# Splitting the diagonal score blocks of a causal attention at 64 queries, and running the matching part of PV as 64-row tiles

## Chip, cores, metric

One core of a Trainium2 chip. The metric is the device time of one execution in microseconds (us), median of several. Times are of fast runs, with a granted TensorE clock of about 1.00. Ratios are the mean time of one kernel's fast runs over the mean of the other's fast runs of the same rounds, so they are not quite the ratio of the medians that I quote.

## The reference, cut to what matters

Sequence 2048, width 512, 32 heads of 16, in four segments of 512 tokens. Each segment does causal softmax attention within itself and reads a linear memory of the earlier segments; a gated FFN of width 1792 runs beside it on the same input.

```python
for s in range(4):                                   # L = 512
    logits = einsum('bhqd,bhkd->bhqk', qs, ks) * scale + mask   # causal within the segment
    a_dot  = einsum('bhqk,bhkd->bhqd', softmax(logits), vs)
    a_mem  = (phi(qs) @ M) / (phi(qs) @ z + 1e-6)
    outs.append(g * a_mem + (1 - g) * a_dot)
    M, z = M + phi(ks).T @ vs, z + phi(ks).sum(...)
a = concat(outs) @ wo
b = (relu(x @ W_gate) * (x @ W_up)) @ W_down
return g2 * a + (1 - g2) * b                         # g2 = sigmoid(x . gate_w)
```

## The kernel before

A static list scheduler in the kernel (with a random seed) orders every operation on every engine beforehand; at run time each engine follows its fixed list and waits on semaphores. FFN and projection matmuls fill PE between the steps of the attention.

Heads come in groups of eight (G). The transposed keys of one parity p of a head pair are kept with the other parity zeroed (`kp`), so that four tiles of 32 rows compute four heads at once. A "quad" is one set of scores of four heads by 512 columns, in four PSUM banks, followed by one exp of 2048 elements a partition:

```python
def quad(tag, parts):                       # parts: (n, key block j, column offset, width)
    for (n, j, o, w) in parts:
        for jj in range(4):
            q.matmul(PL[:, jj, o:o + w], lhsT=V.kp[32*jj:32*jj+32, kslot(s, n), 128*j:128*j+128],
                     rhs=V.qT[32*jj:32*jj+32, qslot(s, n//2), 128*j:512], tile_position=(32*jj, 0), ...)
    a.activation(V.E[:, e, :, :], PL[:, :, :], ACT.Exp, scale=SCALE)           # ScalarE
    for o in offsets:                                                         # GpSimd, 4 x 128 a partition
        g.affine_select(out=V.E[:, e, :, o:o+128], ...)                        # causal mask of the diagonal block
...
# five quads per G: key blocks of 128 keys see 512, 384, 256, 128 queries
eA[0] = quad("A0", [(n0, 0, 0, 512)]);  eB[0] = quad("B0", [(n0, 1, 0, 384), (n0, 3, 384, 128)])
eC    = quad("C",  [(n0, 2, 0, 256), (n1, 2, 256, 256)])
eA[1] = quad("A1", [(n1, 0, 0, 512)]);  eB[1] = quad("B1", [(n1, 1, 0, 384), (n1, 3, 384, 128)])
```

PV of a group comes as a pair, one per parity, with V and a column of ones as the stationary operand, in four tiles of 32 columns:

```python
src = [(eA[p], 0, 512, 0), (eB[p], 0, 384, 128), (eC, 256*p, 256, 256), (eB[p], 384, 128, 384)]
for j, (e, o, w, c) in enumerate(src):
    for jj in range(4):
        q.matmul(A(ep)[32*jj:32*jj+17, c:512], lhsT=V.vaug[:, s % 2, j, 8*G + 2*jj + p, :],
                 rhs=V.E[:, e, jj, o:o+w], tile_position=(0, 32*jj), ...)
```

The softmax here doesn't subtract the row's maximum and nothing guards it: scores larger than these inputs give would overflow.

Of the kernel before, what the change touches and what calls it, by code (L numbers as in the profile page):

```python
# [9 lines left out]
ALU = mybir.AluOpType  # L10
# [78 lines left out]
class Sched:  # L89
# [90 lines left out]

    def _bank_choice(self, op, e):
        cls = op.ep.cls
        if cls != "att":
            held = 0
            nheld = 0
            for prev in self.bank_ep:
                if prev is None or all(r.done for r in prev.readers):
                    continue
                held += prev.cls == cls
                nheld += 1  # L190
            if held >= self.CAPS.get(cls, 2) or nheld >= len(self.bank_ep) - 1:
                return None
        best = None
        for bi, prev in enumerate(self.bank_ep):
            if prev is not None and not all(r.done for r in prev.readers):
                continue
            ft = self._bank_free(prev, e)
            if best is None or ft < best[1]:
                best = (bi, ft)
        return best  # L200
# [166 lines left out]
def plan(S, D, F):  # L367
# [4 lines left out]
        ("qT", [128, 8, 512], BF16), ("kT", [128, 4, 512], BF16), ("kp", [128, 12, 512], BF16),  # L372
        ("phiq", [128, 4, 512], BF16), ("ek", [128, 4, 512], BF16), ("phik", [128, 4, 512], BF16), ("ttmp", [128, 2, 512], BF16),
        ("vaug", [128, 2, 4, 32, 17], BF16), ("E", [128, 8, 4, 512], BF16),
        ("Tn", [128, 2, 512], F32), ("adT", [128, 512], BF16), ("oTt", [128, 512], BF16),
        ("amem", [128, 2, 512], BF16), ("amemT", [128, 4, 512], BF16), ("oT", [128, 8, 512], BF16),
        ("hT", [128, 20, 512], BF16), ("rl", [128, 3, 512], BF16), ("osb", [128, 3, 512], BF16),
# [3 lines left out]
        ("rden", [128, 32], F32), ("rdg", [128, 32], F32), ("rdm", [128, 128], F32), ("pm8", [128, 8], F32), ("pm", [128, 2], F32), ("ident", [128, 128], BF16),  # L381
# [3 lines left out]
def build_kernel(nc, A_x, A_wq, A_wk, A_wv, A_wo, A_beta, W_g, W_u, W_d, gate_w, out):  # L385
# [5 lines left out]
    sc = Sched(seed=59)  # L391
# [14 lines left out]
def program(sc, nc, T, PL, PA, A_x, A_wq, A_wk, A_wv, A_wo, A_beta, W_g, W_u, W_d, gate_w, out, NSEG, KT, NF, NT, EPS, SCALE):  # L406
# [13 lines left out]

    def act(fn, occ, **k):
        return op("act", fn, occ, **k)
# [20 lines left out]
    for nm, w, src in (("wq", V.wq, A_wq), ("wk", V.wk, A_wk), ("wv", V.wv, A_wv)):  # L443
        for kt in range(KT):
            load("act" if nm == "wq" and kt % 2 == 0 else "sp", [f"{nm}{kt}"], w[:, kt, :], src[kt * 128:(kt + 1) * 128, :], 1 << 17)
    load("act", ["gwb"], V.gwb[:], gate_w.partition_broadcast(128), 1 << 17)
# [52 lines left out]
    ds.append(dve(lambda e: e.reduce_sum(V.pm[:, :], pm8, AX.X), 180, reads=["pm8"], writes=["pm"], name="pm"))  # L499
    sc.queue(0, ds)  # L500
# [29 lines left out]
    for s2 in range(2):  # L530
        for tt in range(4):
            cst.append(dve(lambda e, s2=s2, tt=tt: e.tensor_copy(V.vaug[:, s2, tt, :, 16], V.romgh[:, :]), 190, reads=["romgh"], writes=[f"vone{s2}_{tt}"], name="vone"))
# [4 lines left out]
    gq = {"pe": [], "act": [], "dve": [], "flex": [], "pool": [], "sp": []}  # L537
    for c in range(NSEG):
# [17 lines left out]
        gexpT_r[c] = []  # L556
        for a in range(4):
            for jj in range(4):
                dst = V.gexpT[32 * jj:32 * jj + 32, 16 * c + 4 * a:16 * c + 4 * a + 4]
                gq["flex"].append(sc.add(Op([("dve", lambda e, a=a, dst=dst, t0=t0, t1=t1: e.tensor_copy(dst, V.gexp[32 * a:32 * a + 32, t0:t1]), 200),  # L560
                                             ("act", lambda e, a=a, dst=dst, t0=t0, t1=t1: e.activation(dst, V.gexp[32 * a:32 * a + 32, t0:t1], ACT.Copy), 215)],
                                            reads=[f"gexp{c}"], writes=[f"gexpT{c}_{a}{jj}"], name="gexpT")))
                gexpT_r[c].append(f"gexpT{c}_{a}{jj}")
# [8 lines left out]
    sc.queue(2, gq["flex"])  # L572
    sc.queue(3, gq["sp"])

    def kslot(s, n):
        return (s * 8 + n) % 12
# [11 lines left out]
    def proj(s):  # L588
# [3 lines left out]
        def pj(w, col, name, wname, tokmajor=False):  # L592
            ep = Epoch("proj")

            step = 1 if s == 0 and name == "q" and col < 2 else 2
# [9 lines left out]
            return ep  # L605
        for G in range(4):
            ep = pj(V.wq, G, "q", "wq")
            qs = qslot(s, G)
            evs.append(dve(lambda e, ep=ep, qs=qs: e.tensor_copy(V.qT[:, qs, :], A(ep)[:, :]), t_dve(512), writes=[f"qT{qs}"], name=f"qcp{s}_{G}", ep=ep, role="r"))  # L609
# [3 lines left out]
            evs.append(dve(lambda e, ep=ep, G=G: e.tensor_copy(V.kT[:, G, :], A(ep)[:, :]), t_dve(512), writes=[f"kT{G}"], name=f"kcp{s}_{G}", ep=ep, role="r"))  # L613
            for p in range(2):
                ks = kslot(s, 2 * G + p)
                km = lambda e, G=G, p=p, ks=ks: e.tensor_scalar(V.kp[:, ks, :], V.kT[:, G, :], V.pm[:, p:p + 1], None, ALU.mult)  # L616
                ka = lambda e, G=G, p=p, ks=ks: e.activation(V.kp[:, ks, :], V.kT[:, G, :], ACT.Copy, scale=V.pm[:, p:p + 1])
                evs.append(sc.add(Op([("dve", km, 420)] + ([("act", ka, 720)] if s else []), reads=[f"kT{G}", "pm"], writes=[f"kp{ks}"], name=f"kmask{s}_{G}_{p}")))
# [4 lines left out]
        for tt in range(4):  # L623
            ep = pj(V.wv, tt, "v", "wv", True)
            evs.append(dve(lambda e, ep=ep, tt=tt: e.tensor_copy(V.vaug[:, s % 2, tt, :, 0:16], A(ep)[:, :].rearrange("q (h c) -> q h c", c=16)), t_dve(512), writes=[f"va{s % 2}_{tt}"], name=f"vcp{s}_{tt}", ep=ep, role="r"))
        if s == 0:
            pes = [p for k in "qkv" for p in pes if p.name[0] == k]
            pes[:2 * KT] = [pes[h * KT + kt] for kt in range(KT) for h in range(2)]
        return pes, evs, sbs, acts, sps

    def va(s):
        return [f"va{s % 2}_{tt}" for tt in range(4)] + [f"vone{s % 2}_{tt}" for tt in range(4)]

    def mu(s):
        pes, ds, ps = [], [], []
        for hf in range(2):
            ep = Epoch()

            def fn(e, hf=hf, ep=ep):
                for g in range(2):  # L640
                    G = 2 * hf + g
                    for tt in range(4):
                        ins = e.matmul(A(ep)[:, g * 136:(g + 1) * 136], lhsT=V.phik[:, tt, G * 128:(G + 1) * 128], rhs=V.vaug[:, s % 2, tt, 8 * G:8 * G + 8, :], start=(tt == 0), stop=(tt == 3))  # L643
# [38 lines left out]
    e_ctr = [0]  # L682

    carry = []

    def att(s, between):
        pes, acts, pools, ds, pvs = [], [], [], [], []

        def quad(tag, parts):
            e = e_ctr[0]  # L690
            e_ctr[0] = (e + 1) % 8
            wid = max(o + w for (_, _, o, w) in parts)
            assert wid == 512

            def fq(q, parts=parts):
                for (n, j, o, w) in parts:
                    for jj in range(4):
                        ins = q.matmul(PL[:, jj, o:o + w], lhsT=V.kp[32 * jj:32 * jj + 32, kslot(s, n), 128 * j:128 * j + 128],  # L698
                                       rhs=V.qT[32 * jj:32 * jj + 32, qslot(s, n // 2), 128 * j:512], start=True, stop=True, tile_position=(32 * jj, 0), skip_group_check=True)
                return ins  # L700
            rd = [f"kp{kslot(s, n)}" for (n, _, _, _) in parts] + [f"qT{qslot(s, n // 2)}" for (n, _, _, _) in parts]
            pes.append(pe(fq, sum(mm(w) for (_, _, _, w) in parts), reads=rd, writes=[f"bankL{b}" for b in range(4)], name=f"quad{s}_{tag}", mode="r"))
            acts.append(act(lambda a, e=e: a.activation(V.E[:, e, :, :], PL[:, :, :], ACT.Exp, scale=SCALE), t_act(2048), reads=[f"bankL{b}" for b in range(4)], writes=[f"E{e}"], name=f"exp{s}_{tag}"))  # L703
            for o in [o for (_, _, o, _) in parts]:
                ap = V.E[:, e, :, o:o + 128]
                pools.append(pool(lambda g, ap=ap: g.affine_select(out=ap, in_=ap, compare_op=ALU.is_ge, fill=0.0, base=0, pattern=[[0, 4], [1, 128]], channel_multiplier=-1),  # L706
                                  t_pool(512), reads=[f"E{e}"], writes=[f"E{e}m{o}"], name=f"mask{s}_{tag}"))
            return e

        def flush():  # L710
            if not carry:
                return []
            s, G, eA, eB, eC = carry.pop()
            eps = []
            pair = []
            for p in range(2):
                ep = Epoch("att")
                eps.append(ep)

                def fpv(q, p=p, ep=ep):  # L720
                    src = [(eA[p], 0, 512, 0), (eB[p], 0, 384, 128), (eC, 256 * p, 256, 256), (eB[p], 384, 128, 384)]
                    for j, (e, o, w, c) in enumerate(src):
                        for jj in range(4):
                            ins = q.matmul(A(ep)[32 * jj:32 * jj + 17, c:512], lhsT=V.vaug[:, s % 2, j, 8 * G + 2 * jj + p, :], rhs=V.E[:, e, jj, o:o + w],  # L724
                                           start=(j == 0), stop=(j == 3), tile_position=(0, 32 * jj), skip_group_check=True)
                    return ins
                pair.append(pe(fpv, mm(1280), reads=[f"E{x}" for x in (eA[p], eB[p], eC)] + [f"E{eA[p]}m0", f"E{eB[p]}m0", f"E{eB[p]}m384", f"E{eC}m{256 * p}"] + va(s), name=f"pv{s}_{G}_{p}", ep=ep, role="w", mode="c"))
# [15 lines left out]
            else:  # L743
                ds.append(dve(lambda e: e.transpose(V.oTt[:, :], V.adT[:, :]), t_dve(512), reads=["adT"], writes=["oTt"], name=f"bt{s}_{G}"))
                ds.append(dve(lambda e: e.tensor_tensor(V.oT[:, os_, :], V.oTt[:, :], V.amemT[:, G, :], ALU.add), 540, reads=["oTt"] + [f"amemT{i}" for i in range(4)], writes=[f"oT{os_}"], name=f"oa{s}_{G}"))
            return pair

        for G in range(4):
            n0, n1 = 2 * G, 2 * G + 1
            eA, eB = [None, None], [None, None]  # L750
            eA[0] = quad(f"{G}A0", [(n0, 0, 0, 512)])
            eB[0] = quad(f"{G}B0", [(n0, 1, 0, 384), (n0, 3, 384, 128)])
# [3 lines left out]
            eC = quad(f"{G}C", [(n0, 2, 0, 256), (n1, 2, 256, 256)])  # L756
# [176 lines left out]
```

## Time and profile before

| | before |
|---|---|
| time, median | 273.18 us (272.69 to 273.54) |
| span of the profiled run | 271.2 us |
| PE / VectorE / ScalarE / GpSimd busy | 97% / 76% / 75% / 37% |

In the profile PE is TensorE, PEld its weight loads, ACT ScalarE, DVE VectorE and POOL GpSimd. Lines of the page of the kernel before: the busy time of each engine, PE's row over 40 slices, the chain that ended last, and groups of instructions (count, then busy us and mean ns, then idle time before them and its cause).

```profile
span 271.2 us, 5268 instructions
PE 263.0 (97%) x2108; PEld 115.1 (42%) x2143; DVE 204.8 (76%) x382; ACT 203.7 (75%) x210; POOL 99.5 (37%) x156
...
PE   8989999999999999999999999999999999999996
...
PE 88%; ACT 2%; DVE 2%; DMA 2%; issue 2%; POOL 2%; ACTq 1%; DVEq 0%; POOLq 0%
...
L703 ACT ACTIVATE E<-psL 128x2048 bf16<-128x2048 f32 x80 | 150.0, 1875 | 31.1 <-PE psL L698 30.6
L706 POOL TENSOR_SCALAR_AFFINE_SELECT E<-E 128x512 bf16<-128x512 bf16 x128 | 85.4, 685 | 139.6 <-ACT E L703 139.5
```

PE stands at 9, 90% or more, in every slice from the fourth to the last but one, and is 88% of the chain. But a busy PE is not one at its peak, so I went to the starts of the matmuls. Matmul ends are modelled in a trace and overlap; the distance from one start to the next is what an operation costs. This is PE's timeline around one quad and one PV pair of the kernel before (start, length, line, count):

```profile
91.40 1.03 PE L819 MATMUL psA<-wd,hT 128*128 128x512 bf16 x4
92.36 0.40 PE L698 MATMUL psL<-qT,kp 32*128 32x384 bf16 x8
92.69 1.26 PE L724 MATMUL psA<-E,vaug 128*17 128x512 bf16 x32
94.11 0.81 PE L819 MATMUL psA<-wd,hT 128*128 128x512 bf16 x3 [0.16 <-issue]
```

The quad starts at 92.36 and the PV pair at 92.69, 0.33 us later, although the quad streams only 512 columns. (Full-array matmuls of 128 and 512 columns start 56 and 216 ns apart, so a column costs 0.417 ns and 512 columns 213 ns; all streaming times below are worked out with this.) The last full matmul before a quad takes 312 ns to the next start instead of 216. So each quad costs 0.33 + 0.096 = 0.43 us. The FFN matmul recorded at 94.11 is the second one after the pair (35 of the 2143 matmul records are missing; I filled them in from the weight load that follows each, which is always there).

Adding up all start-to-start distances gives a ledger of PE, in us. A stall is the part of a distance above the median of its kind:

| PE from the first projection to the last matmul | before |
|---|---|
| full-array matmuls, memory update and read-out | 207.58 |
| 80 quads: entry 96 ns, then 327 to 330 ns | 33.94 |
| 16 PV pairs: 1206 ns | 19.25 |
| stalls (of these over 25 ns each: 0.98, both before 18 us) | 1.47 |
| **sum** | **262.24** |

There is almost nothing on PE but work.

### The profile page before, as it was taken

The page shows a single profiled execution, that of the slowest core. Times are in us where ns is not written, and L with a number is a line of the kernel's source. Part 1 is how long each engine was busy: PE and PEld are TensorE (multiplying, and loading weights), DVE is VectorE, ACT ScalarE, POOL GpSimd, SP SyncE. Part 2 cuts the span into 40 slices and gives each one's busy share as a digit, 9 for nine tenths or more (in the row PEclk, how much of TensorE's full clock was granted, in tenths as well). Part 3 has the DMA queues.
Part 4 walks back from the last instruction along what each step waited for, and adds up shares of the span by engine and source line. Part 5 has one row for each costly group of instructions (what it writes and reads, how often), then busy time and mean ns, then how long its engine had stood idle before and what let it go on. Part 6 is the DMA issues. An engine that isn't in the chain of part 4 may idle for free.

```text
span 271.2 us, 5268 instructions
## 1 busy us (share of the span) xinstructions
PE 263.0 (97%) x2108; PEld 115.1 (42%) x2143; DVE 204.8 (76%) x382; ACT 203.7 (75%) x210; POOL 99.5 (37%) x156
## 2 busy tenths in 40 slices
PE   8989999999999999999999999999999999999996
PEld 4433343444444444444343444343434444344444
DVE  4689988899889799999888887877773547776300
ACT  3499998898989987899768779887776768682122
POOL 5614343454533253643333532333333242421000
PEclk9999999999999999999999999999999999999999
DMA  6999953102200143210001220000012000000011
GB/s 192 331 365 238 237 96 69 29 7 55 55 25 19 31 89 97 60 39 2 0 2 39 62 78 22 19 2 1 2 39 52 27 19 22 0 0 4 0 39 41
DMA packets 31017, 17.01 MB, mean 63 GB/s; under 512 B 20880, under 2 KB 30992, under 8 KB 30992
## 3 DMA queue, kind: packets, MB, share of 16 engines
q1 hardware_dynamic: 30272, 16.01, 23.3%
q10 hardware_dynamic: 720, 0.66, 1.0%
q8 instruction: 17, 0.28, 0.4%
q14 instruction: 8, 0.07, 0.1%
HBM read 9.84 MB, written 2.10 MB: 44 GB/s over the span
## 4 chain that ended last, share of the span: by engine, by line
PE 88%; ACT 2%; DVE 2%; DMA 2%; issue 2%; POOL 2%; ACTq 1%; DVEq 0%; POOLq 0%
PE psA L780 36%; PE psA L819 17%; PE psL L698 9%; PE psA L602 8%; PE psA L724 7%; PE psA L812 5%; PE psA L600 4%; DMA gwb<-in_gate_w_dram 2%; POOL Tn L543 2%; PE psA L672 1%; PE psA L643 1%; ACT E L703 1%; ACTq L439 1%; DVE osb L828 1%; PE psA L659 0%
## 5 line engine op out<-in xcount | busy, mean ns | idle before, releaser
L703 ACT ACTIVATE E<-psL 128x2048 bf16<-128x2048 f32 x80 | 150.0, 1875 | 31.1 <-PE psL L698 30.6
L706 POOL TENSOR_SCALAR_AFFINE_SELECT E<-E 128x512 bf16<-128x512 bf16 x128 | 85.4, 685 | 139.6 <-ACT E L703 139.5
L780 PE MATMUL psA<-xT,wg 128*128 128x512 bf16 x213 | 58.0, 380 | 1.1 <-issue 0.8
L780 PE MATMUL psA<-xT,wu 128*128 128x512 bf16 x217 | 58.4, 380 | 0.6 <-issue 0.3
L819 PE MATMUL psA<-wd,hT 128*128 128x512 bf16 (+2 forms) x233 | 53.0, 367 | 0.8 <-issue 0.8
L791 DVE TENSOR_TENSOR hT<-psA,rl 128x512 bf16<-128x512 f32 x56 | 38.2, 683 | 13.5 <-PE psA L780 12.5
L698 PE MATMUL psL<-qT,kp 32*128 32x384 bf16 (+3 forms) x512 | 31.7, 301 | 0.8 <-DVE kp L616 0.5
L780 PEld LDWEIGHTS psA<-xT,wu 128*128 128x128 bf16 x224 | 20.4, 98 | 25.8 <-issue 3.2
L819 PEld LDWEIGHTS psA<-wd,hT 128*128 128x128 bf16 x238 | 20.9, 98 | 23.8 <-issue 4.0
L780 PEld LDWEIGHTS psA<-xT,wg 128*128 128x128 bf16 x224 | 20.1, 98 | 24.9 <-issue 3.1
L729 DVE STREAM_TRANSPOSE Tn<-psA 128x512 f32<-128x512 f32 x32 | 20.9, 692 | 7.9 <-PE psA L724 7.9
L789 DVE TENSOR_SCALAR rl<-psA 128x512 bf16<-128x512 f32 x30 | 20.6, 688 | 4.0 <-PE psA L780 3.0
L698 PEld LDWEIGHTS psL<-qT,kp 32*128 32x128 bf16 x512 | 8.9, 92 | 34.0 <-ACT E L703 14.0
L788 ACT ACTIVATE rl<-psA 128x512 bf16<-128x512 f32 x26 | 15.5, 595 | 10.3 <-PE psA L780 10.2
L724 PE MATMUL psA<-E,vaug 128*17 128x256 bf16 (+3 forms) x512 | 20.2, 300 | 0.0
L829 ACT ACTIVATE osb<-psA,omg 128x512 bf16<-128x512 f32 (+2 forms) x10 | 6.4, 645 | 13.7 <-PE psA L812 13.1
L812 PE MATMUL psA<-wo,oT 128*128 128x512 bf16 (+2 forms) x64 | 15.9, 366 | 0.3 <-issue 0.2
L602 PE MATMUL psA<-xT,wk 128*128 128x512 bf16 x62 | 15.9, 380 | 0.2 <-DVE ttmp L585 0.2
L602 PE MATMUL psA<-xT,wq 128*128 128x512 bf16 x61 | 15.5, 380 | 0.5 <-issue 0.3
L600 PE MATMUL psA<-wv,xT 128*128 128x512 bf16 x61 | 14.7, 380 | 0.4 <-issue 0.3
L724 PEld LDWEIGHTS psA<-E,vaug 128*17 128x17 bf16 x512 | 10.7, 90 | 9.4 <-issue 2.5
L609 DVE CAST qT<-psA 128x512 bf16<-128x512 f32 x16 | 10.7, 676 | 3.4 <-PE psA L602 3.3
(71 smaller groups left out, 233.0 us busy)
## 6 DMA issues: line engine op xcount, KB each, us to landing
out_dram<-osb SPq DMA_DIRECT2D x15, 128.0 KB, 1.7
wg<-in_B_W_gate_dram SPq DMA_DIRECT2D x8, 224.0 KB, 5.4
wu<-in_B_W_up_dram SPq DMA_DIRECT2D x8, 224.0 KB, 5.7
wd<-in_B_W_down_dram SPq DMA_DIRECT2D x1, 1792.0 KB, 10.5
osb<-in_A_x_dram SPq DMA_DIRECT2D x12, 128.0 KB, 2.0
wk<-in_A_wk_dram SPq DMA_DIRECT2D x4, 128.0 KB, 5.6
wv<-in_A_wv_dram SPq DMA_DIRECT2D x4, 128.0 KB, 4.9
wo<-in_A_wo_dram SPq DMA_DIRECT2D x1, 512.0 KB, 5.0
```

The source lines that it names most:

```text
L600: ins = e.matmul(A(ep)[:, :], lhsT=V.xT[:, kt, tok + col * 128:tok + (col + 1) * 128], rhs=w[:, kt, :], start=(kt == 0), stop=(kt == KT - 1))
L602: ins = e.matmul(A(ep)[:, :], lhsT=w[:, kt, col * 128:(col + 1) * 128], rhs=V.xT[:, kt, tok:tok + 512], start=(kt == 0), stop=(kt == KT - 1))
L698: ins = q.matmul(PL[:, jj, o:o + w], lhsT=V.kp[32 * jj:32 * jj + 32, kslot(s, n), 128 * j:128 * j + 128], rhs=V.qT[32 * jj:32 * jj + 32, q ...
L703: acts.append(act(lambda a, e=e: a.activation(V.E[:, e, :, :], PL[:, :, :], ACT.Exp, scale=SCALE), t_act(2048), reads=[f"bankL{b}" for b i ...
L706: pools.append(pool(lambda g, ap=ap: g.affine_select(out=ap, in_=ap, compare_op=ALU.is_ge, fill=0.0, base=0, pattern=[[0, 4], [1, 128]], c ...
L724: ins = q.matmul(A(ep)[32 * jj:32 * jj + 17, c:512], lhsT=V.vaug[:, s % 2, j, 8 * G + 2 * jj + p, :], rhs=V.E[:, e, jj, o:o + w], start=(j ...
L729: ds.append(dve(lambda e, p=p, ep=eps[p]: e.transpose(V.Tn[:, p, :], A(ep)[:, :]), t_dve(512), writes=[f"Tn{p}"], name=f"tr{s}_{G}_{p}", e ...
L780: ins = e.matmul(A(ep)[:, :], lhsT=w[:, kt, f * 128:(f + 1) * 128], rhs=V.xT[:, kt, c * 512:(c + 1) * 512], start=(kt == 0), stop=(kt == K ...
L789: ("dve", lambda e, ep=eg, r=r: e.tensor_scalar(V.rl[:, r, :], A(ep)[:, :], 0.0, None, ALU.max), t_dve(512))],
L791: evs.append(dve(lambda e, ep=eu, r=r, hs=hs: e.tensor_tensor(V.hT[:, hs, :], A(ep)[:, :], V.rl[:, r, :], ALU.mult), t_dve(512), reads=[f" ...
L812: ins = e.matmul(A(ep)[:, 0:c1 - c0], lhsT=V.oT[:, o0 + G, i * 128:(i + 1) * 128], rhs=V.wo[:, G, c0:c1], start=st_ and G == 0, stop=sp_ a ...
L819: ins = e.matmul(A(ep)[:, 0:c1 - c0], lhsT=V.hT[:, slots[f], i * 128:(i + 1) * 128], rhs=V.wd[:, f, c0:c1], start=st_ and f == f0, stop=sp ...
```

## The change

The intent: in a 128 x 128 diagonal block, queries 0 to 63 need only keys 0 to 63, so half of the block's first 64 columns is computed and masked away. The change splits each diagonal block at 64 queries. The second halves stay in the quads, whose widths fall to 448, 320, 192 and 64 and pair up to 512: two quads per parity. The first halves of both parities need only 64 keys each, so both share one stationary operand (64 keys of one parity, 64 of the other), and the first halves of two groups fill one shared quad. That makes 4.5 quads per group instead of 5. In PV these first halves have 64 rows per parity, so they run as 64-row, 32-column tiles, eight at a time; V of the second parity has to be shifted to partitions 64 to 127 by a DMA.

```diff
-        ("kT", ...), ("kp", [128, 12, 512], BF16),
+        ("kT", ...), ("kp", [128, 5, 4, 320], BF16),          # [parity 0 | 64 of parity 0 | parity 1]
-        ("hT", [128, 20, 512], BF16),
+        ("hT", [128, 16, 512], BF16), ("vsh", [128, 4, 16, 17], BF16),
...
+        def full(tag, n, blocks):            # two key blocks, second halves and beyond: 64+448 or 192+320 columns
+            for j in blocks:
+                parts.append((*keys(n, j), 128 * j + 64, o, 448 - 128 * j))
+            e = quad(tag, parts)
+            for o in regs:                   # narrow masks, 4 x 64 a partition, on GpSimd
+                ... affine_select(V.E[:, e, :, o:o + 64], base=64) ...
+        def half(tag, G):                    # first halves of both parities, groups G and G+1: 8 parts of 64 columns
+            ... lhsT = V.kp[32 * jj:32 * jj + 32, ks, j, 128:256] ...
+            quad(tag, parts, slot=7)
+            for g in range(2):
+                for h, base in ((64, 0), (128, 64)):       # wide masks: 16 x 64 = 1024 a partition, on GpSimd
+                    ap = half_e(g)[0:h].rearrange("q h (j c) -> q (h j) c", c=64)
+                    ... affine_select(ap, base=base, pattern=[[0, 16], [1, 64]], channel_multiplier=-1) ...
...
-                    src = [(eA[p], 0, 512, 0), (eB[p], 0, 384, 128), (eC, 256 * p, 256, 256), (eB[p], 384, 128, 384)]
+                    src = [(eA[p], 64, 448, 0), (eB[p], 192, 320, 1), (eB[p], 0, 192, 2), (eA[p], 0, 64, 3)]
+                    if p == 1:
+                        for j in (1, 2, 3, 0):
+                            for pp in range(2):
+                                for jj in range(4):
+                                    r = 64 * pp
+                                    v = V.vsh[64:128, j, 4 * G + jj, :] if pp else V.vaug[0:64, s % 2, j, 0, 4 * G + jj, :]
+                                    ins = q.matmul(A(eps[pp])[32 * jj:32 * jj + 17, 128 * j:128 * j + 64], lhsT=v,
+                                                   rhs=half_e(g)[r:r + 64, jj, 64 * j:64 * j + 64], tile_position=(r, 32 * jj), ...)
```

With it came changes around the core: the scheduler's seed (59 to 197), a pace for the quads (one per 3.2 us) and a bank reserved for a PV that is due; projection copies and key masks that may run on either of two engines; additions of the memory part that may run on GpSimd; the 64 small copies of the gate replaced by a DMA through DRAM; the first three q projections interleaved; and `gate_w` loaded ahead of the third slice of `wq`:

```diff
     for kt in range(KT):
+        if nm == "wq" and kt == 2:
+            load("act", ["gwb"], V.gwb[:], gate_w.partition_broadcast(128), 1 << 17)
         load("act" if nm == "wq" and kt % 2 == 0 else "sp", [f"{nm}{kt}"], ...)
-    load("act", ["gwb"], V.gwb[:], gate_w.partition_broadcast(128), 1 << 17)
```

## The prediction

> **What bounds the kernel now.** The tensor engine. The page shows PE busy 263.0 of 271.2 us (97%); the chain of waits is 88% PE; the granted clock is 1.00. From the first projection (6.36 us, timeline) to the last matmul (268.8 us) there are 262.5 us. Start-to-start distances in the trace account for them: 928 full-array matmuls at 216 ns, 200.4 us; memory update and read-out, about 7 us; 80 score quads at about 423 ns, 33.8 us; 16 PV pairs at about 1.3 us with entry, about 20 us. About 2 us of real stalls are left. ScalarE (75%) and VectorE (76%) are not the limit: in the list of waits the quads' weight loads wait for exp (14.0 us), but PE itself waits 0.8 us there.
>
> A quad's 423 ns are 213 ns of streaming, the rest entering (the matmul before it takes 312 ns, not 216) and draining. The Trainium skill, "TensorEngine Tiling (Array Packing)", Key Properties, says a change of tiling mode drains the array; the extra 96 ns agree.
>
> **What the change removes.** 8 of 80 quads and exps: on PE 8 x 423 ns = 3.4 us, on ScalarE 8 x 1.875 = 15.0 us. PV streams 1024 instead of 1280 columns per parity: 213 ns a pair, 3.4 us in all. 57 small gexpT copies (11.6 us) leave ScalarE for a DMA bounce.
>
> **What it adds.** Each PV pair ends in 32 matmuls of 64 rows by 17 columns over 64 queries: another tiling mode, about 100 ns to enter, then four steps of eight concurrent tiles. Streaming is 27 ns a step; neighbouring tiles start 3 ns apart in the trace, with weight loads between, so I estimate 30 to 45 ns a step: 220 to 280 ns a pair. That gives back all that PV saves: net 0 to +1 us. The 8 shared quads have 8 parts of 64 columns: an estimated 80 to 110 ns more each, 0.6 to 0.9 us. Off the path: a third key copy per group, wide POOL masks (POOL is 37% busy), a shift of V by DMA, one buffer for the shared exp block, hT cut from 20 to 16 slots.
>
> **What lies on the critical path.** Only PE time counts: -3.4 + 0.75 + 0.5, about -2.2 us. The relief of ScalarE is almost all off the path; for the new pacing, the bank reserve for PV and the start-up order I allow 0.5 to 1 us. Fewer hT slots and the single shared block could cost as much.
>
> **Prediction.** 270.4 us, -1.0%; 8 in 10 between 267.8 and 272.4. Faster by over 2%: 0.09; within 2%: 0.88; slower by over 2%: 0.03.
>
> **What would show it.** 72 exps of about 1.88 us; ScalarE busy down by 15 us or more while the span falls by under 4; PE 96 to 98% busy; ordinary quads still about 327 ns from first start to the next group, shared quads 400 to 450; PV pairs 1.15 to 1.3 us, their 64-row part 220 to 280 ns; full-array distances 216 ns.
>
> **What would make it wrong.** The 64-row tiles not running concurrently (32 at 27 ns, the spacing of the 8-column matmuls here, would be 860 ns a pair, +10 us); weight loads that a 64-column matmul cannot hide; PV waiting for the wide masks or the V shift; FFN fill running out; or stalls and start-up shrinking more than I see, worth some 3 us at most.

## More of the kernel before

The kernel before was run again beside every experiment, because its median moves between 272.7 and 273.2 us from one set of runs to the next.

The gate of segments 1 to 3 is one VectorE operation with two SBUF inputs per 128 tokens, and the gate of segment 0 a product on GpSimd that ScalarE sums:

```python
e.tensor_tensor_reduce(out=V.osb[:, 2, :], in0=V.osb[:, 2, :], in1=V.gwb[:], ..., accum_out=V.gl[:, t:t+1])   # gate{t}
```

## The result

The changed kernel takes 272.02 us (271.88 to 272.18) beside 273.18: ratio 0.9959 (0.9946 to 0.9971), 1.2 us less by the medians. I had forecast 270.4, 2.8 us less. Lines of the page of the changed kernel that answer to those above:

```profile
span 270.2 us, 6803 instructions
PE 259.7 (96%) x2869; PEld 119.2 (44%) x2911; DVE 192.4 (71%) x349; ACT 185.3 (69%) x160; POOL 128.0 (47%) x209
...
PE   8899999999999999899999999999999999999996
...
PE 84%; DVE 9%; issue 3%; DMA 2%; ACTq 1%; ACT 0%
...
L727 ACT ACTIVATE E<-psL 128x2048 bf16<-128x2048 f32 x72 | 135.0, 1875 | 36.4 <-PE psL L719 36.2
L745 POOL TENSOR_SCALAR_AFFINE_SELECT E<-E 128x256 bf16<-128x256 bf16 x128 | 55.3, 456 | 93.7 <-ACT E L727 91.8
...
L762 POOL TENSOR_SCALAR_AFFINE_SELECT E<-E 64x1024 bf16<-64x1024 bf16 (+1 forms) x32 | 39.0, 1229 | 9.8 <-ACT E L727 8.8
```

ScalarE lost 18 us and VectorE 12 us of work; GpSimd gained 28 us, 39.0 of its 128.0 us being the 32 wide masks of 1.23 us each, which did not exist before. VectorE is now 9% of the chain, from 2%. And the PE row has an 8 in the slice that starts at 108 us, where before it had a 9.

PE's timeline of a PV pair of the changed kernel (the eight lines of the 64-row part cut to two):

```profile
100.22 0.40 PE L719 MATMUL psL<-qT,kp 32*128 32x64 bf16 x8
100.54 1.05 PE L777 MATMUL psA<-E,vaug 128*17 128x448 bf16 x32
101.52 0.20 PE L785 MATMUL psA<-E,vaug 64*17 64x64 bf16 x4
101.54 0.20 PE L785 MATMUL psA<-E,vsh 64*17 64x64 bf16 x4
...
101.99 0.81 PE L889 MATMUL psA<-wd,hT 128*128 128x512 bf16 x3 [0.16 <-issue]
```

The 128-row part takes 0.98 us to the first 64-row start at 101.52: 853 ns of streaming and 128 ns to change the mode. The 64-row tiles run eight at a time. Within a step of eight their starts lie 3.3 ns apart (3.8 ns as the mean of all 32), a step of 64 queries takes 29 ns, and from the first of the 32 to the next full matmul 250 ns pass (median of 16), 132 ns of it after the last start.

The same ledger for both kernels, in us:

| PE | before | after | difference |
|---|---|---|---|
| full-array matmuls, memory update and read-out | 207.58 | 207.71 | +0.13 |
| quads (80; after 64 ordinary and 8 shared) | 33.94 | 30.75 | -3.19 |
| PV pairs (1206 ns; after 981 + 250 ns) | 19.25 | 19.69 | +0.44 |
| stalls | 1.47 | 3.28 | +1.81 |
| **sum** | **262.24** | **261.43** | **-0.81** |

Two tenths more come before the first projection (6.36 to 6.15 us), and the end behind the last matmul is the same (2.6 us): together -1.0 us, the difference of the two spans. So PE's work fell by 2.6 us, about what I had forecast for the whole kernel, and new stalls gave 1.8 us of it back. The stalls over 25 ns are few enough to be listed:

| | where, us | stall, us |
|---|---|---|
| before | 13.94 and 17.80, first two quads | 0.57 and 0.40 |
| after | 6.48 and 8.76, q projection waits for `wq` | 0.11 and 1.20 |
| after | 82.79, an FFN matmul waits for a bank | 0.55 |
| after | 113.64, a q projection waits for a bank | 1.00 |

What happens before the last one, in lines of the timeline of the changed kernel (those of other operations between them are left out):

```profile
109.01 1.14 POOL L762 TENSOR_SCALAR_AFFINE_SELECT E<-E 64x1024 bf16<-64x1024 bf16 x1
109.20 3.72 DVE L566 CUSTOM_DVE_ANT_0 osb<-osb,gwb 128x512 bf16<-128x512 bf16 x1
110.13 1.15 POOL L812 TENSOR_TENSOR oT<-oTt,amemT 128x512 bf16<-128x512 bf16 x1
111.24 3.90 POOL L762 TENSOR_SCALAR_AFFINE_SELECT E<-E 128x1024 bf16<-128x1024 bf16 x3
112.85 0.74 DVE L898 TENSOR_SCALAR osb<-psA,omg 128x512 bf16<-128x512 f32 x1
113.64 1.04 PE L615 MATMUL psA<-xT,wq 128*128 128x512 bf16 x4 [0.93 <-DVE osb L898]
```

The gate operation on VectorE (L566), 0.68 us by its median, takes 3.72 us. It begins while GpSimd is in a wide mask, and ends only after GpSimd has gone through that mask, an addition and another mask. Behind it stands L898, which empties an output bank; PE needs that bank and waits. The addition (L812) also reads SBUF, and it too was let onto GpSimd by the change. At 82.79 us it is the same in small (other lines left out again):

```profile
79.10 5.24 POOL L762 TENSOR_SCALAR_AFFINE_SELECT E<-E 64x1024 bf16<-64x1024 bf16 x4 [0.39 <-ACT E L727]
79.42 0.96 DVE L683 TENSOR_TENSOR rdm<-rdm,c2g 128x128 f32<-128x128 f32 x1
80.43 1.11 DVE L570 TENSOR_SCALAR omg<-gexp 128x4 f32<-128x4 f32 x1
82.05 1.28 DVE L693 TENSOR_TENSOR amem<-psA,rdm 128x512 bf16<-128x512 f32 x2
82.79 1.04 PE L850 MATMUL psA<-xT,wu 128*128 128x512 bf16 x4 [0.38 <-DVE amem L693]
```

Four wide masks in a row stretch a multiplication (L683, 0.26 us at its shortest) to 0.96 us and an addition (L570, 0.16 us at its shortest) to 1.11 us, so that the product that frees PE's bank (L693) comes late.

### The profile page after: what moved, and what is told of

Same layout as the page of the kernel before. It is cut to its first block, busy times and chain, and to the rows that moved or that the text cites. A ratio compares the mean times of both kernels' runs of the same rounds, so it can differ in the third digit from the quotient of the medians.

```text
span 270.2 us, 6803 instructions
## 1 busy us (share of the span) xinstructions
PE 259.7 (96%) x2869; PEld 119.2 (44%) x2911; DVE 192.4 (71%) x349; ACT 185.3 (69%) x160; POOL 128.0 (47%) x209
## 4 chain that ended last, share of the span: by engine, by line
PE 84%; DVE 9%; issue 3%; DMA 2%; ACTq 1%; ACT 0%
PE psA L850 35%; PE psA L889 16%; PE psA L615 9%; PE psL L719 8%; PE psA L777 5%; PE psA L882 4%; PE psA L613 4%; DMA wq<-in_A_wq_dram 2%; DVE osb L566 1%; PE psA L785 1%; PE psA L689 1%; DVE osb L898 1%; DVE Tn L796 1%; PE psA L660 1%; ACTq L451 1%
## 5 line engine op out<-in xcount | busy, mean ns | idle before, releaser
L727 ACT ACTIVATE E<-psL 128x2048 bf16<-128x2048 f32 x72 | 135.0, 1875 | 36.4 <-PE psL L719 36.2
L745 POOL TENSOR_SCALAR_AFFINE_SELECT E<-E 128x256 bf16<-128x256 bf16 x128 | 55.3, 456 | 93.7 <-ACT E L727 91.8
L889 PE MATMUL psA<-wd,hT 128*128 128x512 bf16 (+2 forms) x227 | 51.9, 366 | 1.4 <-issue 1.3
L762 POOL TENSOR_SCALAR_AFFINE_SELECT E<-E 64x1024 bf16<-64x1024 bf16 (+1 forms) x32 | 39.0, 1229 | 9.8 <-ACT E L727 8.8
L858 ACT ACTIVATE rl<-psA 128x512 bf16<-128x512 f32 x31 | 18.5, 597 | 21.1 <-PE psA L850 20.7
L719 PE MATMUL psL<-qT,kp 32*128 32x64 bf16 (+3 forms) x768 | 28.7, 245 | 0.0
L719 PEld LDWEIGHTS psL<-qT,kp 32*128 32x128 bf16 x768 | 9.9, 92 | 29.2 <-issue 19.1
L859 DVE TENSOR_SCALAR rl<-psA 128x512 bf16<-128x512 f32 x25 | 17.2, 686 | 4.6 <-PE psA L850 4.0
L777 PE MATMUL psA<-E,vaug 128*17 128x192 bf16 (+3 forms) x512 | 16.8, 273 | 0.0
L812 POOL TENSOR_TENSOR oT<-oTt,amemT 128x512 bf16<-128x512 bf16 x9 | 10.4, 1152 | 8.7 <-DVE oTt L811 8.7
## 6 DMA issues: line engine op xcount, KB each, us to landing
out_dram<-osb SPq DMA_DIRECT2D x15, 128.0 KB, 1.7
osb<-in_A_x_dram SPq DMA_DIRECT2D x12, 128.0 KB, 2.3
wk<-in_A_wk_dram SPq DMA_DIRECT2D x4, 128.0 KB, 5.8
wv<-in_A_wv_dram SPq DMA_DIRECT2D x4, 128.0 KB, 5.1
```

The lines of the kernel that those rows point to most:

```text
L719: ins = q.matmul(PL[:, jj, o:o + w], lhsT=kap(jj), rhs=V.qT[32 * jj:32 * jj + 32, qs, q0:q0 + w], start=True, stop=True, tile_position=(32 ...
L727: acts.append(act(lambda a, eout=eout: a.activation(eout, PL[:, :, :] if slot is None else PL[:, :, :].rearrange("q h (g c) -> q h g c", g ...
L745: pools.append(pool(lambda g, ap=ap: g.affine_select(out=ap, in_=ap, compare_op=ALU.is_ge, fill=0.0, base=64, pattern=[[0, 4], [1, 64]], c ...
L762: pools.append(pool(lambda e, ap=ap, base=base: e.affine_select(out=ap, in_=ap, compare_op=ALU.is_ge, fill=0.0, base=base, pattern=[[0, 16 ...
L777: ins = q.matmul(A(eps[p])[32 * jj:32 * jj + 17, 512 - w:512], lhsT=V.vaug[:, s % 2, j, p, 4 * G + jj, :], rhs=V.E[:, e, jj, o:o + w], sta ...
L889: ins = e.matmul(A(ep)[:, 0:c1 - c0], lhsT=V.hT[:, slots[f], i * 128:(i + 1) * 128], rhs=V.wd[:, f, c0:c1], start=st_ and f == f0, stop=sp ...
```

## Theories

**Theory 1, a shared port.** The Trainium skill, "SBUF — State Buffer", section "Who interferes with whom", says that VectorE and GpSimd share a port pair. A VectorE operation with two SBUF inputs contends with a GpSimd operation that reads SBUF, one in a two-port fast mode contends with any GpSimd operation, and whichever comes second waits for the other's whole instruction. Then the wide masks are the cause, through VectorE, and about 1.5 us of the loss is theirs. The other 0.3 us is start-up.

**Theory 2, start-up.** The largest single stall, 1.20 us at 8.76 us, is the price of loading `gate_w` ahead of `wq`'s third slice, and would come back if the order were put back.

**Theory 3, the order.** The stalls are a draw of the static order: another seed would have none.

**Theory 4, PE's tile work** costs more than the ledger says (the 64-row tiles above all), or **ScalarE** paces the attention.

## Experiments

Where an edit is made after scheduling, or only inside an operation, every engine keeps the order of the kernel it was made from.

### e1: the load order put back (theory 2)

```diff
     sc.run()
+    pa = sc.prog["act"]                       # ScalarE's program
...                                            # k0, k1: the places of the loads of gate_w and of wq's third slice
+    pa[k0], pa[k1] = pa[k1], pa[k0]
```

> The changed kernel; only the order of two loads on the ScalarE queue is put back, wq's third slice ahead of gate_w; the programs of PE, VectorE, GpSimd and SyncE are the same. Theory: PE's 1.20 us wait at 8.76 us for wq is the price of that order and lies on the critical path: the wait falls under 0.3 us and the time by 0.8 to 1.1 us, to 270.9 to 271.2. Rival: the wait is only moved, the next dependency (key copies, the first exps, the FFN weights) takes it up: under 0.3 us gained.

Correct; 272.23 us, 0.9982 (0.9967 to 0.9997) of the kernel before: no gain at all. The stall at 8.8 us is gone, and a stall of 1.09 us stands at 11.74 us. PE in e1's timeline (GpSimd's product, the sum on ScalarE and the copy of q behind it come between the two lines and are not shown):

```profile
9.78 1.03 PE L615 MATMUL psA<-xT,wk 128*128 128x512 bf16 x4
11.74 1.90 PE L615 MATMUL psA<-xT,wk 128*128 128x512 bf16 x8 [0.93 <-ACT qT L620]
```

The copy of q that frees the bank is on ScalarE, behind a sum over `x * gate_w` that now starts later. The rival was right: the start-up has two loads that are both needed first, and either order costs a good microsecond.

### e4: the kernel before with `gate_w` early (theory 2, from the other side)

The same swap in the kernel before.

> The kernel before with gate_w loaded ahead of wq's third slice, as the change has it; nothing else. Theory: PE then waits 1.0 to 1.5 us for wq near 8.8 us and the kernel takes 0.9 to 1.4 us longer, 274.1 to 274.6. Rival: within 0.3 us of the kernel before.

Correct; 273.47 us beside 272.72, 1.0026 (1.0013 to 1.004), so 0.75 us longer by the medians. PE now waits 1.16 us for `wq` at 8.70 us, but the two stalls of the first quads (0.98 together) have vanished: stalls grow by only 0.18 us. Another 0.32 us of this trace is a later first projection (6.68 instead of 6.36 us). The theory fell between the two expectations: the wait is there, but most of it replaces another. In all four arrangements up to here (before, after, e1, e4) the start-up stalls come to 0.98 to 1.31 us.

### e2: narrow masks (theory 1)

Result wrong on purpose.

```diff
-                    ap = half_e(g)[0:h].rearrange("q h (j c) -> q (h j) c", c=64)
+                    ap = half_e(g)[0:h].rearrange("q h (j c) -> q (h j) c", c=64)[:, 0:2, :]
-                    ... pattern=[[0, 16], [1, 64]] ...
+                    ... pattern=[[0, 2], [1, 64]] ...
```

> The changed kernel with the 32 masks of the shared block cut from 1024 to 128 elements a partition (result wrong on purpose; schedule the same). Theory: the wide GpSimd masks hold VectorE operations up, these hold banks back from PE: PE's stalls at 82.8 us (0.55) and 113.6 us (1.0) vanish, the 3.72 us gate operation at 109.2 us falls to about 0.9, time down 1.2 to 1.6 us to 270.4 to 270.8. Rival: those stalls come from ScalarE or from the narrow bank reserve: no change (within 0.3 us).

270.39 us, 0.9914 (0.99 to 0.9929). Both late stalls are gone; the only stall over 25 ns left is the one at start-up (0.90 us). The gate operation at that place takes 0.65 us. PE's ledger falls from 261.4 to 259.5 us.

### c1: control

The changed kernel again, beside the next three runs.

> Control: the changed kernel itself, unaltered, to have it on the same chip as the three runs beside it. Both theories: ratio to the kernel before 0.994 to 0.998, the same three PE stalls near 8.8, 82.8 and 113.6 us.

Correct; 271.92 us, 0.9953 (0.9941 to 0.9965); stalls at 8.66 (0.93), 82.72 (0.55) and 113.59 us (1.01). The late stalls are therefore no accident of one execution. The start-up stalls do vary: here they are 0.97 us together (0.93, and 0.04 at 17.01), as much as in the kernel before; in the first execution of the changed kernel they were 1.31.

### e3: the gate with one SBUF input (theory 1, mechanism)

Result wrong on purpose.

```diff
-    e.tensor_tensor_reduce(out=V.osb[:, 2, :], in0=V.osb[:, 2, :], in1=V.gwb[:], ..., accum_out=V.gl[:, t:t + 1])
+    e.reduce_sum(V.gl[:, t:t + 1], V.osb[:, 2, :], AX.X)
```

> The changed kernel with the gate's multiply-and-sum on VectorE (two SBUF inputs) replaced by a plain sum over one SBUF input of the same size (result wrong on purpose; schedule the same). Theory, a port shared by VectorE's second SBUF input and GpSimd: no gate operation is longer than 0.8 us whatever GpSimd does (now up to 3.72), the stall at 113.6 us (1.0) vanishes, the one at 82.8 us (0.55, other operations) stays; time down 0.8 to 1.1 us. Rival, VectorE is slowed by any traffic of GpSimd: the sum at 109.2 us is stretched as well, time within 0.3 us of the changed kernel.

270.90 us, 0.9935 (0.9919 to 0.9952). The same stretch of e3's timeline:

```profile
108.64 1.14 POOL L762 TENSOR_SCALAR_AFFINE_SELECT E<-E 64x1024 bf16<-64x1024 bf16 x1
108.83 0.64 DVE L566 TENSOR_REDUCE gl<-osb 128x1 f32<-128x512 bf16 x1
109.75 1.14 POOL L812 TENSOR_TENSOR oT<-oTt,amemT 128x512 bf16<-128x512 bf16 x1
110.86 3.44 POOL L762 TENSOR_SCALAR_AFFINE_SELECT E<-E 128x1024 bf16<-128x1024 bf16 x3
110.94 0.75 DVE L898 TENSOR_SCALAR osb<-psA,omg 128x512 bf16<-128x512 f32 x1 [1.47 <-PE psA L889]
```

In the middle of the same masks the sum takes 0.64 us, and the longest of its twelve takes 0.681. L898 even waits for PE now. The stall at 113.6 us is gone, and the one at 82.5 us (0.54), which hangs on other operations, has stayed. That is theory 1 in detail, place by place. (The sum also no longer writes the 512 products back; e5, which leaves this operation as it is, tells the two apart.) The gain by the ratio, 0.2% against the control or 0.5 us, is less than the 1.0 us that the trace shows; by the medians it is 1.0 us. The two belong to different sets of runs. In e3's own set e1, which keeps both late stalls, takes 272.23 us, 1.3 us more.

### e5: masks that do not read (theory 1, mechanism)

Result wrong on purpose.

```diff
-    e.affine_select(out=ap, in_=ap, compare_op=ALU.is_ge, fill=0.0, ...)
+    e.memset(ap, 1.0)
```

> The changed kernel with the 32 wide masks turned into memsets of the same 1024 elements: GpSimd is as busy but does not read SBUF there (result wrong on purpose, schedule the same). Theory, a read port shared by GpSimd and VectorE's second SBUF input: the gate operation at 109.2 us, held up by three GpSimd operations (3.72 us), falls under 1.9 us, the stall at 113.6 us vanishes; one-input operations in a fast mode (the 0.16 us addition at 80.4 us) may still wait. Time down by 0.8 to 1.6 us against the changed kernel in the same job. Rival, any GpSimd write or mere bandwidth: the gate stays over 3 us, time within 0.3 us.

270.55 us, 0.9903 (0.989 to 0.9916), 1.4 us under the control by the medians. By the traces some 0.3 us of this is a shorter start-up stall. GpSimd is nearly as long at it (0.95 us each by the median, where a wide mask takes 1.15), in the same places:

```profile
108.11 0.94 POOL L762 MEMSET E<- 64x1024 bf16 x1
108.31 0.65 DVE L566 CUSTOM_DVE_ANT_0 osb<-osb,gwb 128x512 bf16<-128x512 bf16 x1
...
109.02 1.15 POOL L812 TENSOR_TENSOR oT<-oTt,amemT 128x512 bf16<-128x512 bf16 x1
110.11 2.99 POOL L762 MEMSET E<- 128x1024 bf16 x3
```

The two-input gate operation is not held up by a memset; both late stalls are gone, and only the start-up stall (0.65 us) is left. So it is GpSimd's *reading* that keeps a two-input VectorE operation waiting, as the page has it. A one-input VectorE operation in a fast mode does wait for a memset: the first `ttmp` operation (a `tensor_scalar` over 1024 elements) takes 1.20 us beside one, 0.41 us alone, which also agrees with the page.

### s1: another seed (theory 3)

```diff
-    sc = Sched(seed=197)
+    sc = Sched(seed=46)
```

> The changed kernel with another seed of its static scheduler (46 for 197); every operation and its cost the same, only the order on each engine differs. Theory: PE's tile work is 2.8 us lower whatever the order, and what is given back is stalls that the order decides, since the scheduler knows nothing of the lock between VectorE and GpSimd. I replayed the orders of 61 seeds with durations from the trace and with the lock; this seed came out 1.7 us below 197. Expected 270.0 to 270.9 us, PE stalls over 25 ns together under 1.8 us (2.85 with 197). Rival: the extra time is in PE's own tile work: any order gives 272 within 0.4 us.

Correct; 272.29 us, 0.9985 (0.996 to 1.001; one of the six runs took 274.43 us at a granted clock of 0.994 and widens the interval). A miss: no faster than seed 197. Its late stalls are other ones (0.35 us at 120.78 us, about 0.27 at 36.22, 0.24 at 31.09, and two smaller); the start-up stall is 1.15 us; stalls over 25 ns come to 2.2 us against 2.53 in the control, and PE's last matmul starts only 0.43 us earlier. My replay of the order put a gain of 1.7 us on it; it was too coarse for that. Nor does this support theory 4: PE's tile work was the same, as the theory said (981 ns and 241 ns for the two parts of a PV pair, as in the control). In this one draw, changing the order alone exchanged stalls and did not remove their cause; other seeds by themselves were not tried.

### e6: the 64-row part twice (theory 4)

Result wrong on purpose.

```diff
-                        for j in (1, 2, 3, 0):
+                        for rp, j in [(rp, j) for rp in range(2) for j in (1, 2, 3, 0)]:
...                                            # and start and stop moved to the first and the second pass
```

> The changed kernel with the 64-row part of PV run twice in a row (result wrong on purpose), to measure it by itself: 32 more matmuls a pair. Theory, eight tiles run at once and a step of 64 queries takes 26 to 30 ns: from the first 64-row matmul to the next full one 250 ns become 354 to 370 ns, 16 pairs cost 1.7 to 1.9 us more. My prediction's upper estimate of 45 ns a step would be 2.9 us. Rival, no concurrency: 32 x 27 = 860 ns a pair, 13.8 us more.

277.93 us, 1.0185 (1.0168 to 1.0202). A miss for every number expected: from the first 64-row matmul to the next full one it is now 603 ns. In the control, whose trace like this one lacks no matmul record, it is 241 ns (250 in the first trace of the changed kernel), so the second pass cost 362 ns. The starts in the trace show how: the first 32 lie 3.8 ns apart on average, as in the changed kernel; then comes a gap of 104 ns, and the second 32 lie 8.3 ns apart. The 27 ns spacing of the rival is out, but so is repetition as a measure: a second pass does not cost what the first one costs. Each pass is 32 weight loads and 32 matmuls. The Trainium skill, "TensorE: Matmul & The Clock Gate", section "Architectural detail: the array is 16× 32×32, not 1× 128×128", gives the engine a queue of 64; that a full queue carries the first pass and the second must be fed is a guess that no run here tests. For the change itself the direct reading stands: 250 ns in place of 213 ns of streaming saved.

### e7: half the exp in the kernel before (theory 4, ScalarE)

Result wrong on purpose.

```diff
-    a.activation(V.E[:, e, :, :], PL[:, :, :], ACT.Exp, scale=SCALE)
+    hw = 512 if qn[0] <= 8 else 256
+    a.activation(V.E[:, e, :, 0:hw], PL[:, :, 0:hw], ACT.Exp, scale=SCALE)
```

> The kernel before with 72 of its 80 exps over half the columns only: about 0.85 us less each, some 60 us of ScalarE work gone, far more than the change takes away (result wrong on purpose, schedule the same). Theory, ScalarE is off the critical path: at most the 0.4 us stall before the second quad could go, and that exp is still whole: time within 0.5 us of the kernel before. Rival, the exp rate paces the attention: several us faster.

273.12 us, 1.0005 (0.9992 to 1.0017). The line of the page, to be read beside the one of before:

```profile
PE 263.3 (97%) x2108; PEld 115.1 (42%) x2143; DVE 202.2 (74%) x382; ACT 144.1 (53%) x210; POOL 97.7 (36%) x156
```

Sixty microseconds less of ScalarE, and nothing gained. So in the kernel before ScalarE is off the path, and the 18 us that the change takes off it are worth nothing by themselves.

### v1, v2, v3: repairs

In all three, the four wide GpSimd masks of a shared quad become two VectorE multiplications by a 0/1 tile, one for both parities:

```diff
-                for h, base in ((64, 0), (128, 64)):
-                    ap = half_e(g)[0:h].rearrange("q h (j c) -> q (h j) c", c=64)
-                    ... gpsimd affine_select(ap, ...) ...
+                ap = half_e(g).rearrange("q h (j c) -> q (h j) c", c=64)
+                ... vector tensor_tensor(ap, ap, V.hmask[:, :].unsqueeze(1).to_broadcast([128, 16, 64]), ALU.mult) ...
```

v2 and v3 also put `gate_w` behind `wq` again, and hold the sums of the first gate on ScalarE back, so that they no longer stand before the copy of q (`gad.after = 16000.0` in the scheduler). v3 keeps the additions of the memory part on VectorE. Each has a seed of its own, 38, 21 and 41, picked by the same replay.

> A correct repair: the four wide GpSimd masks of a shared block become two VectorE multiplications by a 0/1 tile (an estimated 0.7 us each), GpSimd busy falls by some 36 us to about 92; seed 38, whose replay has few stalls. Theory: without the wide masks VectorE is not held up for long and PE's stalls after the start-up are under 0.4 us: 270.2 to 270.9 us, faster than the changed kernel by 1.1 to 1.8. Rival: VectorE's 11 us of new work makes stalls of its own: 271.5 or more.

Correct; 271.36 us, 0.994 (0.9927 to 0.9954). After the start-up only one stall over 25 ns is left (0.15 us), as expected, and PE's ledger is 260.1 us, 1.3 less than the changed kernel's. But the start-up stall was 1.16 us, plus 0.12, and the time is worse than I expected; by the ratio it is only just below the control. Part of this lies outside the profiled span. v1's span is 269.0 us by the median, 1.2 less than the changed kernel's 270.2, but the time less the span is 2.3 us in v1 and 1.7 to 1.9 in every run of the changed kernel and the kernel before (2.1 to 2.2 in v2, 1.8 to 2.1 in v3). Why, no trace here shows.

> As the repair before it, and also gate_w loaded after all of wq with the gate's sums on ScalarE held back to 16 us, so that they do not stand in front of the copy of q; seed 21. Theory: the start-up stall of about 1.0 to 1.2 us falls under 0.4, the time to 269.3 to 270.2. Rival: something else takes the start-up up again, as it did when only the load order was put back: 270.3 or more.

Correct; 270.28 us, 0.9899 (0.9884 to 0.9913). Its span and busy times on the page:

```profile
span 268.3 us, 6793 instructions
PE 259.4 (97%) x2871; PEld 119.4 (44%) x2911; DVE 191.3 (71%) x359; ACT 187.8 (70%) x166; POOL 91.5 (34%) x180
```

And PE in the first 13 us of its timeline:

```profile
6.61 3.61 PE L619 MATMUL psA<-xT,wq 128*128 128x512 bf16 x16 [0.86 <-DMA wq<-in_A_wq_dram]
10.06 2.75 PE L619 MATMUL psA<-xT,wk 128*128 128x512 bf16 x11
12.75 0.40 PE L723 MATMUL psL<-qT,kp 32*128 32x64 bf16 x8
```

GpSimd is back at 34%. The first projection waits for `wq` and starts at 6.61 us (6.15 in the changed kernel), but then the 16 q projections run without a gap, k follows, and there is no start-up stall over 25 ns. Three stalls over 25 ns are left in the whole kernel, 0.55 us together, and the ledger is 259.1 us.

> As the last one, and the additions of the memory part are kept on VectorE (10 us less GpSimd work, 4 us more VectorE work); seed 41. Theory: GpSimd busy about 82 us, fewest long waits of VectorE; 269.3 to 270.3 us. Rival: VectorE becomes the one that holds banks back: 270.5 or more.

Correct; 270.24 us, 0.9908 (0.9888 to 0.9927); stalls of 0.60 us. No different from v2 within the interval; the time is at the upper end of what I expected. Both beat the kernel before by about 1.0% and the changed kernel by about 0.5% (0.9899 and 0.9908 against 0.9953 and 0.9959, from different sets of runs).

## Why the prediction was right or wrong

The measured time, 272.02, lies within the range, but the saving is 1.2 us where I forecast 2.8. That the time fell inside the range is owed to the range's width: the 1.5 us lost behind the masks stood nowhere in my sum.

- **What bounds the kernel: right.** PE is 97% and 96% busy, and taking 60 us off ScalarE (e7) changes nothing.
- **The drain at a mode change: right.** 96 ns before a quad and 128 ns between the 128-row and 64-row tiles. The statement of the Trainium skill, "TensorEngine Tiling (Array Packing)", Key Properties, agrees.
- **Quads saved: right, with one term mis-sized.** The 64 ordinary quads are unchanged (327 to 330 ns). A shared quad of eight parts takes 345 ns, 16 more, not the 80 to 110 that I put on it. Quads save 3.2 us, half a microsecond more than I had counted.
- **PV gives its saving back: right.** The 64-row part takes 250 ns (I had 220 to 280), the pair 1.23 us (1.15 to 1.3), net +0.4 us (0 to 1.0). The tiles do run eight at a time.
- **Fill, masks before PV, the V shift: harmless, as hoped.** No stall over 25 ns stands before a PV or lacks fill.
- **The step that failed: "Off the path: ... wide POOL masks (POOL is 37% busy)", and with it "for the new pacing, the bank reserve for PV and the start-up order I allow 0.5 to 1 us" of gain.** GpSimd has time enough, but while it reads SBUF a two-input VectorE operation stands still. VectorE's copies free PE's banks, and two such delays cost PE 1.54 us. e2, e3 and e5 show it from three sides. The stalls did not shrink by 0.5 to 1 us: they grew by 1.8, the remaining 0.3 at the start-up. There the new load order (1.31 us of stalls) took the place of the first quads' waits (0.98), and e1 and e4 show that exchanging the two loads only moves the wait. This 0.3 us is not safe: in the control the start-up stalls are 0.97 us, no more than before.

Without the stalls my sum would have held: v2, with the same tile work (981 and 249 ns for the two parts of a PV pair) and 0.55 us of stalls, runs in 270.28 us; I had predicted 270.4. It is a different order with a different mask, so this supports the sum and does not prove it.

What stays open: how a waiting VectorE operation could be passed over twice by GpSimd at 109.2 us, while elsewhere it got in after one; how much of v1's small gain is the order and how much the mask; and why v1 and v2 take 0.4 to 0.5 us more outside the profiled span. The pacing of the quads, the bank reserve, the fewer hT slots and the gate's DMA were not varied one by one; the ledger leaves them nothing but the stalls listed.

## What to carry to other kernels

When one engine is full and the rest have slack, price the full engine's work from start-to-start distances, and then ask what the moved work will *hold up*: 39 us of new masks on a GpSimd that had been 37% busy cost 1.5 us, because they blocked the engine that frees the banks of the full one. A stall is not always a cost that can be taken out singly: removing the largest one (1.2 us) gained nothing (e1), because its twin stood behind it; v2, which removed both (with another seed), ran 1.1 us faster than v1. Prove a stall's cause by making the same operation, in the same place and order, unable to have it (one input instead of two, a write instead of a read).

## What the Trainium skill lacked or had wrong

- "SBUF — State Buffer", "Who interferes with whom": right in all that e2, e3 and e5 tested. It says that the second to issue is blocked until the first finishes; here a gate operation of 0.68 us was passed over by two further GpSimd operations and took 3.72 us. The page has nothing on back-to-back GpSimd operations keeping the port.
- "TensorEngine Tiling (Array Packing)", Key Properties: no figure for a change of mode. Here 96 ns into the 32-row mode, about 117 ns out of it (330 ns less 213 of streaming), 128 ns from 128-row to 64-row column tiles, and 132 ns from the last 64-row start to the next full one.
- The same page, "Instruction Overhead", gives some 60 cycles to each matmul; it does not say that tiles which run side by side do not pay it one after the other: within a step of eight their starts lie 3.3 ns apart here. "TensorE: Matmul & The Clock Gate", "Measured speedup vs the span model", has about 4 ns a tile, which fits.
- No page has what e6 showed: after 32 such matmuls with their weight loads, a gap of 104 ns and then 8.3 ns a matmul on average instead of 3.8.
- No page that I read has a figure for a moving operand that is read in short runs: the memory update's 136-column matmuls went from 59 to 63 ns when V was laid out by parity, so that each reads eight runs of 17 elements from two places in turn.
